# First queries in two loads by pairs of heads, the small term as a 33rd element, six idle products fewer

## The chip, the cores and the metric

The kernel runs on one core of a Trainium2 chip. A core has five engines that work side by side, each with a queue of its own: TensorE (PE in the profile; its weight loads are PEld), VectorE (DVE), ScalarE (ACT), GpSimd (POOL) and SyncE (SP), which here issues most of the transfers. Transfers run on 16 DMA engines. Data lie in SBUF, 128 partitions wide; products are written to PSUM, which has eight banks. The metric is the device time of one execution in microseconds (us), as the median of several runs.

## The reference

Inputs are q, k, v (8 batches, 8 heads, 576 positions, 64 wide), phi (the same, 32 wide) and the weights of a mixture of eight experts over rows of 512.

```
a    = exp(phi - max(phi));  a = a / (sum(a) + 1e-9)          # over the 32
k_m  = a^T k ;  v_m = a^T v                                    # 32 x 64 for each head
s    = q k_m^T / 8 ;  s = exp(s - max(s));  s = s / (sum(s) + 1e-9)   # over the 32
x    = s v_m                                                   # rows of all heads side by side: 4608 x 512
e    = argmax(x w_gate + bias[modality]) ;  g = softmax weight of e
out  = g * (relu(x w1[e]) w2[e])                               # 512 -> 1024 -> 512
```

So each batch first makes 32 "memory" keys and values for each head out of phi, k and v, then softens 576 queries against them, and the resulting rows pass an expert. The 1e-9 is what the text calls the small term.

## The kernel before, in words

**Tiling.** A batch has 8 heads; they are held as 2 groups (NG, on the two halves of the partitions) of 4 heads (HG, along the free dimension). The 576 positions of a head are 64 partitions times 9 columns (QC). The columns of a batch are worked on in two parts, RA = 4 columns and RB = 5 columns. The expert is guessed on the chip from the bias alone, so that its weights can be loaded early; where the guess proves wrong in the end, a slower path follows, which is not taken with these inputs. Products whose precision matters are made three times, from upper and lower halves of the operands (names ending in h and l).

**Order.** Each engine works strictly in the order in which the kernel wrote its instructions. That order is made by a small planner, `weave()`: a list of steps for attention and one for the experts, each step with its predecessors and with estimated times (`TAKES`). The steps of the first batch are laid down by `plan_first()` in a fixed sequence; a step of the kind "nothing" has no estimated time, and `nothing(n)` writes n products whose result nobody reads. Behind the start the planner mixes attention of the next batches into the products of the experts.

**The start.** Ahead of everything the kernel writes, in this order: the loads of phi (halves from SP and ACT), k, v and the first part of the first queries on SP's queue; on PE, `warm_small(BUSY[0])` (small products on a tile of zeros) and `warm(BUSY[1])` (large ones); and small fills on GpSimd. Then `plan_first()`:

- the maximum of phi (`heads_max`, L305), its transposition on PE (`mem_top`, `turn` at L147), the guess of the expert on VectorE (L211 to L217) and, from SP, the loads of w1, of w2, and of the rest of the first queries (`guess`, L218 to L238);
- `mem_exp` (L363 to L373): subtraction on VectorE and exponential on ScalarE, in three parts by columns;
- `spread_row` (L250), `mem_sums` (L384 to L387) on VectorE;
- `first_products(0)` (L428) on PE, the keys; `first_sums` (L439); `first_divide` (L448 to L465), which ends with the even halves on ScalarE;
- the transposition of the queries on VectorE, `q_turn` (L547), heads 0 and 1; `first_odd(0)` (L472), the keys; `q_turn`, heads 2 and 3; on PE `first_products(1)` (L428), the values;
- `first_keys` (two transpositions on PE, L147, and a copy on ScalarE, L526), `first_scores` (L574);
- `soften` for each of the two groups (L601 transposition out of PSUM, L605 maximum, L607 subtraction, L609 exponential) and `first_weights` (L642 sum, L643 small term, L644 reciprocal, L646 product, L650 transposition), then `first_split` (L656, L658);
- between them the value weights out of w1 (L740, L749, L754, L757, L762) and the first hidden tiles (`hidden`, L787, and `relu`, L800 and L804); after those the first outputs (L824), which need w2's halves (`first_w2`: L863 on ScalarE, L864 on GpSimd).

In VectorE's order the lines that matter are:

```
turns(0, 0, 9.5)                                   # q_turn, heads 0 and 1
add(("ko", 0), "ko0", [("kn", 0)], first_odd, 0)   # the keys
turns(0, 1, 11.0)                                  # q_turn, heads 2 and 3
```

The remaining columns of the first queries are turned later (L547 again, `turns(1, ...)`), ahead of the second `first_scores`.

Of the kernel before, what the change touches and what calls it, by code (L numbers as in the profile page):

```python
# [8 lines left out]
F32 = mybir.dt.float32  # L9
# [45 lines left out]
def attn_moe(ctx: ExitStack, tc: tile.TileContext, q, k, v, phi, mod_id, w_gate, mod_bias, w1, w2, out):  # L55
# [20 lines left out]
    HW = MAIN + 2 * QP  # L76
    SCALE = 1.0 / float(D) ** 0.5
    EPS = 1e-9
    BUSY = 92, 10

    FAR = float(1 << 20)

# [87 lines left out]
    def halves(src, b):  # L170
        return src[b].rearrange("(j g) (p c) d -> (g p) j (c d)", g=NG, c=QC)
# [7 lines left out]
    def load_queries(b, c0=0, n=QC):  # L179
        if b == 0:  # L180
            cols = slice(c0 * D, (c0 + n) * D)
            nc.sync.dma_start(q_sb[b % 2][:, :, cols], halves(q, b)[:, :, cols])
            return
        src = q[b].rearrange("(j g) (t x) (u d) -> g u j t x d", g=NG, t=BL, u=2)
        for g in range(NG):
            for u in range(2):
                p0 = QP * g + BL * u
                to = q_sb[b % 2][p0:p0 + BL].rearrange("t j (x d) -> t j x d", d=BL)
                for j in range(HG):
                    later.append((to[:, j], src[g, u, j]))  # L190
# [396 lines left out]
    def by_token(x, n, inner):  # L587
        return x[:, 0:2 * NG * n * inner].rearrange("p (g a c m) -> p g a c m", a=2, g=NG, c=n)

    def soften(b, part, step=None, groups=None):  # L590

        n = rows_of(part)
        if step in (None, 0) and groups in (None, 0):
            live["a", b, part] = by_token(wk.tile([P, 2 * NG * RB * M], F32, name="a", bufs=2), n, M)
            live["mx"] = by_token(wk.tile([P, 2 * NG * RB], F32, name="mx", bufs=2), n, 1)
        a, mx, sc = live["a", b, part], live["mx"], live["sc", b]
        for gs in groups_of(b, part) if groups is None else [slice(groups, groups + 1)]:
            x, m = (y[:, gs].rearrange("p g a c m -> p (g a c) m") for y in (a, mx))
            if step in (None, 0):
                for g in range(gs.start, gs.stop):  # L600
                    nc.vector.transpose(  # L601
                        a[:, g].rearrange("p a c m -> p a (c m)"), sc[g][:, :, RA * part * BL:(RA * part + n) * BL]
                    )
            if step in (None, 1):
                nc.vector.tensor_reduce(m[:, :, 0], x, axis=AX.X, op=ALU.max)  # L605
            if step in (None, 2):
                nc.vector.tensor_tensor(x, x, m.broadcast_to(list(x.shape)), op=ALU.subtract)  # L607
            if step in (None, 3):
                nc.scalar.activation(x, x, AF.Exp, scale=SCALE)  # L609
# [25 lines left out]
    def first_weights(g, step):  # L635
# [3 lines left out]
        n = 2 * RA  # L639
        if step == 0:  # L640
            sa, ra = (wk.tile([P, 2 * NG * RB], F32, name=y, bufs=2)[:, 0:n] for y in ("sa", "ra"))
            nc.vector.tensor_reduce(sa, x, axis=AX.X, op=ALU.add)  # L642
            nc.vector.tensor_scalar_add(sa, sa, EPS)  # L643
            nc.vector.reciprocal(ra, sa)  # L644
            ra = ra.rearrange("p (x o) -> p x o", o=1)
            nc.vector.tensor_tensor(x, x, ra.broadcast_to(list(x.shape)), op=ALU.mult)  # L646
            return
# [283 lines left out]
    def plan_first():  # L931
# [27 lines left out]
        add(("top", 0), "top0", [("max", 0)], mem_top, 0)  # L959
        add(("preferred",), "guess", [], preferred)  # L960
        add(("guess",), "guess", [], guess)
        nothing(1)
        add(("exp", 0), "first exp", [("top", 0)], mem_exp, 0)
        nothing(4)
        add(("known",), "nothing", [], spread_row)
        add(("sums", 0), "first sums", [("exp", 0)], mem_sums, 0)
        add(("k", 0), "k0", [("exp", 0)], first_products, 0, floor=9.0)
# [255 lines left out]
    with tc.manual_schedule():  # L1223
# [9 lines left out]
        load_queries(0, 0, RA)  # L1233
        warm_small(BUSY[0])
        warm(BUSY[1])
        nc.gpsimd.memset(ones_c, 1.0)
        ones_r = wk.tile([1, P], F32, name="ones_r")
        nc.gpsimd.memset(ones_r, 1.0)
# [133 lines left out]
```

## Time and profile before

| | |
|---|---|
| median of 3 runs | 391.02 us (390.63 to 391.76) |
| profiled execution | 391.15 us, span 389.0 us |
| PE busy | 376.1 us, 97% of the span |
| VectorE busy | 245.3 us, 63% |
| ScalarE busy | 140.5 us, 36% |
| GpSimd busy | 45.7 us, 12% |
| chain that ended last | PE 92%, DMA 3%, DVE 2% |
| mean granted clock of TensorE | 0.996 |

How to read the rows. A row of the timeline or of the chain starts with the start and the length in us, counted from the span's start, then engine, line of the kernel, operation, what it writes and reads, the shape and how often; in brackets the idle time of the engine ahead of it and what ended it. SPq and ACTq are the queues that issue transfers. A row of the transfers gives the size in KB and the us from issue to landing. A row of the windows gives the stretch, its length, for PE, PEld, DVE, ACT and POOL the busy us and the number of instructions, then PE's granted clock, the share of the DMA engines' time and GB/s. A row of waits gives who waited for whom, the us in total, how often and the longest. The time of an execution is longer than its span by what lies around it.

### The profile page before, as it was taken

How to read it: one execution, taken by the hardware profiler on the slowest of the kernel's cores; microseconds unless marked ns; L12 is line 12 of the kernel's file. 1: busy time of each engine (PE TensorE's matmuls, PEld its weight loads, DVE VectorE, ACT ScalarE, POOL GpSimd, SP SyncE). 2: the span in 40 equal slices, each digit the busy share in tenths (PEclk: the TensorE clock that was granted, in tenths of full speed). 3: DMA queues.
4: the chain of work that ended last, by engine and by line, in shares of the span. 5: the costliest groups of instructions: out<-in, count | busy, mean ns of one | idle time of the engine just before them, and what ended most of it. 6: DMA issues, size and time to landing. Idle time of an engine off the chain costs nothing.

```text
span 389.0 us, 9842 instructions
## 1 busy us (share of the span) xinstructions
PE 376.1 (97%) x3987; PEld 302.1 (78%) x3988; DVE 245.3 (63%) x613; ACT 140.5 (36%) x327; POOL 45.7 (12%) x112
## 2 busy tenths in 40 slices
PE   7899999999999999989999999999999999999992
PEld 3577876889679797877879877787968887798982
DVE  4788758867787397735686479654774635880400
ACT  2382423534335153423433334341543242441310
POOL 3247030040000300030000300021000030000000
PEclk9999999999999999999999999999999999999998
DMA  8998679978750588419611096816311010171111
GB/s 294 349 376 207 102 122 310 281 199 294 162 102 29 177 232 209 164 24 341 111 35 56 9 346 108 293 29 205 95 29 50 7 42 16 27 272 30 28 42 48
DMA packets 91451, 56.89 MB, mean 146 GB/s; under 512 B 69252, under 2 KB 74628, under 8 KB 91396
## 3 DMA queue, kind: packets, MB, share of 16 engines
q1 hardware_dynamic: 90976, 55.74, 51.0%
q8 instruction: 33, 0.54, 0.6%
q10 hardware_dynamic: 420, 0.43, 0.3%
q14 instruction: 22, 0.18, 0.1%
HBM read 37.28 MB, written 18.87 MB: 144 GB/s over the span
## 4 chain that ended last, share of the span: by engine, by line
PE 92%; DMA 3%; DVE 2%; issue 1%; ACT 0%; SPq 0%; ACTq 0%
PE pe L824 53%; PE pe L787 26%; PE pair L403 4%; PE pe L740 4%; DMA q_sb<-in_q_dram 3%; PE pair L556 2%; PE pair L687 1%; PE pair L574 1%; PE pair L147 1%; PE pair L536 0%; PE pair L411 0%; SPq L177 0%; DVE a L646 0%; DVE aT L650 0%; DVE mx L605 0%
## 5 line engine op out<-in xcount | busy, mean ns | idle before, releaser
L824 PE MATMUL pe<-w2h,hh 128*128 128x512 f32 x288 | 117.2, 407 | 0.0
L824 PE MATMUL pe<-w2h,hl 128*128 128x512 f32 x288 | 112.6, 391 | 0.0
L824 PE MATMUL pe<-w2l,hh 128*128 128x512 f32 x288 | 110.6, 392 | 0.0
L804 DVE SCALAR_TENSOR_TENSOR hl<-pe,hh 128x256 fp32r<-128x256 f32 (+2 forms) x158 | 57.5, 390 | 38.6 <-ACT hh L800 37.7
L824 PEld LDWEIGHTS pe<-w2h,hh 128*128 128x128 f32 x288 | 54.1, 188 | 23.8 <-issue 13.8
L800 ACT ACTIVATE hh<-pe 128x256 fp32r<-128x256 f32 (+2 forms) x158 | 53.2, 361 | 37.2 <-PE pe L787 36.5
L824 PEld LDWEIGHTS pe<-w2l,hh 128*128 128x128 f32 x288 | 54.0, 188 | 11.8
L824 PEld LDWEIGHTS pe<-w2h,hl 128*128 128x128 f32 x288 | 54.2, 188 | 9.4
L837 ACT ACTIVATE ob<-pe,gates 128x512 f32<-128x512 f32 x35 | 23.9, 687 | 76.4 <-PE pe L824 44.0
L787 PE MATMUL pe<-xbh,vwh 128*128 128x320 f32 x128 | 40.3, 315 | 0.0
L787 PE MATMUL pe<-xbh,vwl 128*128 128x320 f32 x128 | 39.6, 309 | 0.0
L787 PE MATMUL pe<-xbl,vwh 128*128 128x320 f32 x128 | 39.6, 309 | 0.0
L787 PE MATMUL pe<-xah,vwh 128*128 128x256 f32 x124 | 35.3, 287 | 0.9 <-ACT xah L656 0.9
L787 PE MATMUL pe<-xal,vwh 128*128 128x256 f32 x124 | 34.9, 283 | 0.0
L787 PE MATMUL pe<-xah,vwl 128*128 128x256 f32 x124 | 34.9, 283 | 0.0
L339 POOL COPY ts<-tm 32x4 f32<-32x4 f32 x24 | 4.8, 199 | 205.6 <-DVE tm L331 204.9
L787 PEld LDWEIGHTS pe<-xah,vwh 128*128 128x128 f32 x124 | 23.6, 192 | 3.2 <-ACT xah L656 2.0
L152 ACT CAST vwh<-pe 128x512 fp32r<-128x512 f32 x26 | 14.0, 590 | 32.1 <-PE pe L740 32.1
L787 PEld LDWEIGHTS pe<-xbh,vwh 128*128 128x128 f32 x128 | 24.0, 188 | 1.2 <-DVE hl L804 0.6
L787 PEld LDWEIGHTS pe<-xbl,vwh 128*128 128x128 f32 x128 | 24.1, 188 | 0.3
L787 PEld LDWEIGHTS pe<-xbh,vwl 128*128 128x128 f32 x128 | 24.0, 188 | 0.0
L787 PEld LDWEIGHTS pe<-xal,vwh 128*128 128x128 f32 x124 | 23.7, 192 | 0.2
(173 smaller groups left out, 440.6 us busy)
## 6 DMA issues: line engine op xcount, KB each, us to landing
kv_sb<-in_k_dram SPq DMA_DIRECT2D x8, 1152.0 KB, 6.9
kv_sb<-in_v_dram SPq DMA_DIRECT2D x8, 1152.0 KB, 9.2
out_dram<-ob SPq DMA_DIRECT2D x65, 128.0 KB, 2.6
q_sb<-in_q_dram SPq DMA_DIRECT2D x112, 72.0 KB, 3.1
ph<-in_phi_dram SPq DMA_DIRECT2D x7, 576.0 KB, 10.2
raw<-in_moe_w_dram SPq DMA_DIRECT2D x2, 1024.0 KB, 7.1
raw<-in_moe_w_dram SPq DMA_DIRECT2D x1, 1280.0 KB, 10.7
out_dram<-ob SPq DMA_DIRECT2D x3, 256.0 KB, 2.0
```

The costliest lines, as they stand in the source:

```text
L147: nc.tensor.transpose(dst, src, ident[:rows, :rows])
L152: nc.scalar.copy(h, src)
L339: nc.gpsimd.tensor_copy(ts_[BL * a:BL * (a + 1)], live["tm"][BL * o:BL * (o + 1)])
L403: nc.tensor.matmul(live["kvp"][M * j:M * (j + 1), g], lhsT=pe[half, j, c * M:(c + 1) * M], rhs=kv_sb[half, :, j, c * D:(c + 1) * D], start ...
L556: nc.tensor.matmul(sc[g][M * j:M * (j + 1), a, 0:QC * BL], lhsT=kvT[b][rows, 0, M * j:M * (j + 1)], rhs=qT[rows, j, a], start=True, stop=T ...
L574: nc.tensor.matmul(sc[g][M * j:M * (j + 1), a, c0 * BL:(c0 + n) * BL].rearrange("p (c t) -> p c t", t=BL), lhsT=kT0[p0:p0 + BL, u, M * j:M ...
L740: nc.tensor.matmul(pvs[g][M * j:M * (j + 1), :], lhsT=vT[b][rows, j, :], rhs=raw1[rows, j, cols], start=True, stop=not more, tile_position ...
L787: nc.tensor.matmul(ph[:, 0:n], lhsT=(vl if k == 2 else vh)[:, g, cols], rhs=xl if k == 1 else xh, start=(g == k == 0), stop=(g == NG - 1 a ...
L800: nc.scalar.activation(hs[0][:, f, h0:h0 + p1 - p0], live["ph", f][:, p0:p1], AF.Relu)
L804: nc.vector.scalar_tensor_tensor(hl, live["ph", f][:, p0:p1], 0.0, hh.bitcast(F32), op0=ALU.max, op1=ALU.subtract)
L824: nc.tensor.matmul(po, lhsT=tile_columns(hl if n == 1 else hh, f, t), rhs=(w2l if n == 2 else w2h)[:, f, :], start=(f == n == 0), stop=(f ...
L837: nc.scalar.activation(ob, po, AF.Copy, scale=gate_of(b, t))
```

## The change

Three things are changed in the start of the kernel; the order of all other instructions is left alone.

1. The first part of the first queries (4 columns of all heads) is loaded by two transfers in place of one: heads 0 and 1 of each group, then heads 2 and 3. The rest of these queries is loaded by one transfer as before.
2. The weights of the first part get a tile of their own, `a0`, 33 elements wide in place of 32. GpSimd fills the 33rd column with the small term at the start. The four steps of `soften` and the product and transposition of `first_weights` work on the first 32 columns; the sum runs over all 33, and the separate addition (L643) goes.
3. Six products of nothing go: one of the 92 small ones, one behind `preferred` and `guess`, four behind `mem_exp`, ahead of the keys.

```diff
-    BUSY = 92, 10
+    BUSY = 91, 10
...
         if b == 0:
             cols = slice(c0 * D, (c0 + n) * D)
-            nc.sync.dma_start(q_sb[b % 2][:, :, cols], halves(q, b)[:, :, cols])
+            for js in (slice(0, HG // 2), slice(HG // 2, HG)) if c0 == 0 else (slice(0, HG),):
+                nc.sync.dma_start(q_sb[b % 2][:, js, cols], halves(q, b)[:, js, cols])
             return
...
         if step in (None, 0) and groups in (None, 0):
-            live["a", b, part] = by_token(wk.tile([P, 2 * NG * RB * M], F32, name="a", bufs=2), n, M)
+            live["a", b, part] = live["a0"][:, :, :, :, 0:M] if b == part == 0 else by_token(
+                wk.tile([P, 2 * NG * RB * M], F32, name="a", bufs=2), n, M
+            )
...
                     nc.vector.transpose(
-                        a[:, g].rearrange("p a c m -> p a (c m)"), sc[g][:, :, RA * part * BL:(RA * part + n) * BL]
+                        a[:, g] if b == part == 0 else a[:, g].rearrange("p a c m -> p a (c m)"), sc[g][:, :, RA * part * BL:(RA * part + n) * BL]
                     )
...
             sa, ra = (wk.tile([P, 2 * NG * RB], F32, name=y, bufs=2)[:, 0:n] for y in ("sa", "ra"))
-            nc.vector.tensor_reduce(sa, x, axis=AX.X, op=ALU.add)
-            nc.vector.tensor_scalar_add(sa, sa, EPS)
+            whole = live["a0"][:, g].rearrange("p a c m -> p (a c) m")
+            nc.vector.tensor_reduce(sa, whole, axis=AX.X, op=ALU.add)
             nc.vector.reciprocal(ra, sa)
...
         add(("guess",), "guess", [], guess)
-        nothing(1)
         add(("exp", 0), "first exp", [("top", 0)], mem_exp, 0)
-        nothing(4)
         add(("known",), "nothing", [], spread_row)
...
         warm(BUSY[1])
+        live["a0"] = wk.tile([P, NG, 2, RA, M + 1], F32, name="a0")
+        nc.gpsimd.memset(live["a0"][:, :, :, :, M:M + 1], EPS)
         nc.gpsimd.memset(ones_c, 1.0)
```

## The prediction

> **What bounds the kernel now.** I read the page first, for its span, and then the waits of PE alone from 23.8 us to the end, to see whether anything behind the start can absorb or add time.
>
> ```profile
> span 389.0 us, 9842 instructions
> ```
>
> ```profile
> PE pair L411 <- issue: 1.3, 1, 1.3
> PE pe L787 <- ACT xah L656: 0.9, 1, 0.9
> ```
>
> In 365 us PE waits twice. One wait, at L787, is the end of the start: the last products of the first hidden tiles wait for the second group of first weights. The other (L411) is a pause of 1.3 us that no engine causes. All else is one unbroken row of products. So whatever reaches PE earlier at L787 arrives at the end in full, as long as no transfer that keeps its own time gets in between; a change ahead of L787 that isn't on the way to it is worth nothing.
>
> The way to L787 is read from the chain of waits in order of time (start, length, what):
>
> ```profile
> 2.29 11.05 DMA q_sb<-in_q_dram
> ...
> 14.77 0.44 PE pair L147 x2
> 15.24 0.38 ACT kT L526
> 15.66 1.05 PE pair L574 x54
> 16.74 0.46 DVE a L601
> ...
> 19.27 0.18 DVE sa L643
> 19.48 0.21 DVE ra L644
> ...
> 20.25 0.46 DVE aT L650
> ...
> 21.95 0.18 DVE sa L643
> 22.16 0.21 DVE ra L644
> ...
> 23.79 0.51 PE pe L787 x2
> ```
>
> It starts with the load of the first queries, landed at 2.29 + 11.05 = 13.34 us. Then come VectorE's transposition of the queries, the keys, the key transposition on PE (L147), its copy (L526), the scores (L574), and from 16.74 us VectorE without a pause worth naming. Both additions of the small term (L643) lie on this chain. Why the queries hold up the keys is in the timeline of that stretch:
>
> ```profile
> 11.38 0.29 DVE L387 TENSOR_TENSOR sums<-sums,t2top 128x128 f32<-128x128 f32 x1
> 11.73 0.29 PE L439 MATMUL pair<-ones_c,sums 64*64 64x1 f32 x8
> 11.88 2.20 PE L428 MATMUL pe<-kv_sb,exp 64*64 64x128 f32 x72
> ...
> 12.48 0.16 DVE L452 TENSOR_TENSOR recs<-rec,places 128x4 f32<-128x4 f32 x1
> 12.74 0.52 ACT L465 ACTIVATE even<-pair,recs 128x64 f32<-128x64 f32 x2 [2.46 <-DVE recs L452]
> 13.37 0.71 DVE L547 STREAM_TRANSPOSE q_sb<-q_sb 128x512 f32<-128x512 f32 x1 [0.72 <-DMA q_sb<-in_q_dram]
> ...
> 14.00 0.82 DVE L472 SCALAR_TENSOR_TENSOR keys<-pair,recs,even 128x64 f32<-128x64 f32 x4
> 14.73 0.70 DVE L547 STREAM_TRANSPOSE q_sb<-q_sb 128x512 f32<-128x512 f32 x1
> ```
>
> VectorE is free at 12.64 us, but next in its order is the transposition of heads 0 and 1, and that waits 0.72 us for the whole load of four heads. Behind it in the same queue stand the four key instructions, whose inputs (the even halves) are there at 13.26 us.
>
> **The split load.** The one transfer of 512 KB (128 partitions, 4 heads, 1 KB pieces) becomes two of 256 KB, in the same order on the same queue. What lies ahead of them stays as it is, and so does the total of bytes. The DMA engines are full in this stretch:
>
> ```profile
> 12.00:14.00 2.00, 2.00 (x75) 1.84 (x72) 1.12 (x4) 0.52 (x2) 0.00 (x0) 1.00 1.05 383
> ```
>
> At 383 GB/s (last column) half of the load, 0.262 MB, is 0.68 us. So heads 0 and 1 land at 12.66 us and heads 2 and 3 at 13.34 as before. The transposition then starts at 12.69 us (now, too, it starts 0.03 us behind the landing; VectorE is free at 12.64), against 13.37: **0.68 us** less. It hands over after 0.63 us (13.37 to 14.00), so the keys start at 13.32 us, just behind the even halves' 13.26; no more than 0.74 us could be had here. The second transposition comes at 14.05 us, 0.7 us behind its own landing. PE's key transposition moves from 14.77 to 14.09 us, where the value products, which end at 11.88 + 2.20 = 14.08 us, are just left behind: this is the next limit, and what is asked fits by 0.01 us. L526 and L574 follow at the same distance; L574 at 14.98 us finds the second half of the queries done at 14.05 + 0.70 = 14.75. The second issue stands on SP's queue right behind the first, where SP has nothing else to do until the choice of the expert (first issue after it at 9.31 us, below); it costs the path nothing there.
>
> [...]
>
> **The 33rd element.** The scores' first part gets a tile of its own, 33 wide, whose last column holds the small term; the sum then runs over 264 elements instead of 256 and L643 goes, once for each of the two groups. By the chain, L643 takes 19.27 to 19.48 and 21.95 to 22.16: 0.21 us each. Against it stands the longer sum:
>
> ```profile
> 18.83 0.41 DVE L642 TENSOR_REDUCE sa<-a 128x8 f32<-128x256 f32 x1
> ```
>
> Eight elements more are at most 8/256 of 0.41 us, 0.01 us. That leaves 0.20 us each, **0.40 us** together, both on the chain, the second because ScalarE and PE wait for it at L787. The transpositions, the maximum, the subtraction and the exponential now walk rows 33 apart. No row shows that step. The nearest are the two transpositions of the same size, one written as it comes (L601, 0.46 us) and one into a scattered order (L650, 0.46 us): no difference, so I take nothing. From the other side, if each of the seven VectorE passes of a group were 5% longer, the 0.40 us would shrink to about 0.1. The one new fill on GpSimd stands ahead of its other small fills, and the wait of GpSimd for the modality ids hides it; without that cover it would be one fill of 16 elements, which L643's 0.21 us bounds.
>
> **Six products of nothing fewer.** One of 92 small ones (0.01 us), one behind the transposition of the maxima, and four ahead of the keys' products. What bounds the path here is VectorE: the keys' sums end at 11.38 + 0.29 = 11.67 us and the sums' products (L439) start at 11.73. The keys' products stand in PE's order ahead of L439; if they begin earlier, PE waits for the same L387. Worth nothing, unless the array's clock suffers, which is a rival below.
>
> **What is late next.** Transfers keep their times while all else comes 1.08 us earlier. I compare each landing (issue plus time to landing) with its first user:
>
> ```profile
> 9.31 0.40 SPq L222 DMA_DIRECT2D raw<-in_moe_w_dram  x1
> ...
> 12.30 1.10 SPq L227 DMA_DIRECT2D raw<-in_moe_w_dram  x1
> ...
> 17.46 0.43 SPq L182 DMA_DIRECT2D q_sb<-in_q_dram  x1
> ```
>
> ```profile
> raw<-in_moe_w_dram SPq DMA_DIRECT2D x1, 1024.0 KB, 7.1
> ```
>
> ```profile
> raw<-in_moe_w_dram SPq DMA_DIRECT2D x1, 1280.0 KB, 10.7
> ```
>
> ```profile
> q_sb<-in_q_dram SPq DMA_DIRECT2D x1, 640.0 KB, 10.0
> ```
>
> ```profile
> 17.35 1.13 PE L740 MATMUL pair<-raw,kvT 64*32 64x512 f32 x16 [0.35 <-ACT kvT L531]
> 24.12 0.62 ACT L863 CAST w2h<-raw 128x512 fp32r<-128x512 f32 x1
> ...
> 27.80 0.84 DVE L547 STREAM_TRANSPOSE q_sb<-q_sb 128x640 f32<-128x640 f32 x1
> ...
> 28.86 0.82 DVE L547 STREAM_TRANSPOSE q_sb<-q_sb 128x640 f32<-128x640 f32 x1
> ...
> 30.59 1.18 PE L574 MATMUL pair<-q_sb,kT 32*32 32x160 f32 x64
> ```
>
> The first half of w1 lands at 16.4 us and is wanted at 17.35 - 0.68 = 16.67: in time by 0.2. The second half has no landing in the trace; w2's 1.31 MB behind it end at 23.0 us and take 3.4 us at 383 GB/s, so it is there at about 19.6 us, perhaps a few tenths late for its products (L740 again, further on). PE has 0.9 us to spare there, since it waits at L787 afterwards. w2 lands at 23.0 us and its first cast moves to 24.12 - 1.08 = 23.04: a tie. The rest of the first queries lands at 27.46 us, and VectorE would want it at 26.7. Here VectorE will **wait 0.75 us** at L547, with one lower half of the hidden tiles, the second transposition and a maximum of the next phi queued behind. The second transposition then ends at about 29.4 us (27.5 + 1.06 to its start + 0.82), and PE wants it for the scores at 30.59 - 1.08 = 29.5. So this wait is swallowed by a distance that shrinks from 0.9 us to 0.1; I charge 0.03 us and keep 0 to 0.3 for the range.
>
> **Sum.** 0.68 + 0.40 - 0.03 = 1.05 us. The profiled execution took 391.15 us (span 389.0 and 2.1 us around it) and would take 390.10; it lies 0.13 us above the median of the three runs, 391.02, so against that median the forecast is **389.97 us**.
>
> **Rivals.** First, *the halves don't part*: the transposition of heads 0 and 1 waits for both, or the first half's last engine lands late. [...] Against it: the rest of these queries shares the tile with them, lands at 27.46 us, and the transposition at 13.37 us doesn't wait for it. Only 0.40 us would be left: 390.6 us.
>
> Second, *the transfers take it back*: the landing at 27.46 us or w2's at 23.0 comes a few tenths later than now, or the wide rows cost their 5%. The distance left over is 0.1 us, so each further tenth goes straight into PE's scores. With 0.3 to 0.6 us lost it gives 390.3 to 390.6, say 390.4 us.
>
> Third, on the other side, *the clock of the array falls* in the pause that the missing products leave, and the products of keys and values run at half speed. The times of products of nothing and the busy time by window (PE first, clock the third column from the end):
>
> ```profile
> 3.12 3.62 PE L158 MATMUL pair<-busy 128*128 128x512 bf16 x8 [0.22 <-issue]
> ...
> 8.04 1.04 PE L158 MATMUL pair<-busy 128*128 128x512 bf16 x4
> ```
>
> ```profile
> 13.66:17.07 3.41, 2.17 (x83) 1.29 (x75) 2.60 (x9) 0.84 (x4) 0.19 (x2) 1.00 1.11 295
> 6.84:10.25 3.41, 2.99 (x40) 1.73 (x44) 2.70 (x9) 1.48 (x4) 0.69 (x7) 1.00 1.03 381
> ```
>
> Such a product starts every 0.43 us at first and every 0.22 us at 8 us, so the array was at half speed at first, whatever the clock column says of that time. Without the four (1.04 us) and the single one (about 0.25) the stretch from 6.84 to 10.25 us would have some 1.7 us of PE in place of 2.99, half, and a pause of about 1 us in one piece. For the rival: the row of 13.66 to 17.07 us, which stays fast, has more, 2.17 us, two thirds. Against it: that stretch, too, holds pauses of 0.7 and 0.45 us (14.08 to 14.77 and 15.21 to 15.66). If the clock fell, the keys' products, of the same number and form as the values', would take 4.4 instead of 2.20 us from about 9.4 (11.73 - 2.2) and end at 13.8; the values' products, at full speed again by then, would end at about 16.2 with L439 between, and the key transposition would start at 16.2 instead of 14.77. That is 1.4 us lost against 0.40 won: 391.02 + 1.0 = 392.0 us. It decides once the fall comes early enough to slow more than half of the keys' products, ahead of about 10.5 us.
>
> Fourth, *each transfer pays its own start in line*. The bound is the smallest transfer that the page lists alone:
>
> ```profile
> out_dram<-ob SPq DMA_DIRECT2D x65, 128.0 KB, 2.6
> ```
>
> Of its 2.6 us to landing, 0.131 MB at 383 GB/s are 0.34; if the other 2.3 us stood in line, the second half would land at 15.6 us, its transposition would end at 16.35, and the scores would start 0.7 us later than now: 391.02 + 0.7 - 0.40 = 391.3 us. Against it: the engines' share of 1.05 in the window above leaves no room for such gaps between the transfers that already stand in this queue. [...]
>
> **How the numbers follow.** The forecast gets 0.62, the halves that don't part 0.08, the transfers that take it back 0.16, the falling clock 0.09, the start in line 0.03, and 0.02 remain for a larger gain than I see. The forecast's own range is 389.5 to 390.3. The range reaches from there over the first two rivals, 389.4 to 391.0, and leaves the clock and the start in line out. A measurement of this kernel can tell about 0.3% from no change, 1.17 us: faster means below 389.85, slower above 392.19. The forecast lies only 0.12 us from that bound, so half of its 0.62 counts as faster: 0.31 + 0.02 = 0.33. Slower is 0.06 of the falling clock's 0.09, since it can hit a second stretch. The rest is no change, 0.61.
>
> **What would show it.** L547's first row would start near 12.69 us with a wait of less than 0.1, the keys at 13.32, L574 near 14.98. Each L644 (renumbered) would follow the sum directly, and L787's wait would end near 22.7. The load of the rest would show as a wait of about 0.75 us at L547 near 26.7, and PE would still have no other wait. The forecast is wrong if L787 moves by 1.1 us and the span doesn't, if the transposition still waits until 13.3, or if the products of the keys take longer than 2.2 us.

## The result, and the profile after

The changed kernel takes **389.34 us** (median of 5 runs, 388.08 to 389.78) against 391.02 us before: a ratio of 0.9946, 95% interval 0.9922 to 0.997. That is faster by 1.7 us where 1.05 were forecast, and below the range, which began at 389.4. Almost nothing of it came the way the prediction had it. In the rows below the lines are renumbered (L411 is L412, L428 is L429, L547 is L548, L642 is L646, L740 is L743, L787 is L790); the kernels of the experiments have numbers of their own, up to 10 apart.

The page of the changed kernel, and the waits of PE from 9 us on (who waited for whom, us in total, how often, longest):

```profile
span 387.9 us, 9830 instructions
...
PEclk9899999999999999999999999999999999999998
```

```profile
PE pair L429 <- ACT exp L374: 0.6, 1, 0.6
PE pair L575 <- ACT kT L527: 0.5, 1, 0.5
PE pair L743 <- ACT kvT L532: 0.4, 1, 0.4
```

The two waits that the prediction named are both gone: the 0.9 us at L787, and the pause of 1.3 us at L411, which no engine caused and which the prediction had held fixed. The second digit of the clock's row is an 8. The windows of that stretch (PE first, granted clock third from the end):

```profile
6.40:9.81 3.41, 1.83 (x26) 1.12 (x28) 2.70 (x10) 1.07 (x3) 0.98 (x8) 1.00 1.05 387
9.82:13.22 3.40, 3.40 (x79) 3.40 (x74) 1.68 (x5) 0.43 (x2) 0.00 (x0) 0.50 1.07 370
```

PE was busy for 1.83 of 3.41 us, and in the next 3.40 us its clock was half. The timeline of VectorE and PE in the start of the changed kernel:

```profile
9.31 3.69 PE L429 MATMUL pair<-kv_sb,exp 64*64 64x128 f32 x72 [0.62 <-ACT exp L374]
...
13.18 0.16 DVE L449 TENSOR_SCALAR den<-pair 128x2 f32<-128x2 f32 x1 [1.54 <-PE pair L440]
...
13.65 0.71 DVE L548 STREAM_TRANSPOSE q_sb<-q_sb 128x512 f32<-128x512 f32 x1
14.39 0.86 DVE L473 SCALAR_TENSOR_TENSOR keys<-pair,recs,even 128x64 f32<-128x64 f32 x4
...
17.77 1.09 PE L743 MATMUL pair<-raw,kvT 64*32 64x512 f32 x16 [0.35 <-ACT kvT L532]
...
19.26 0.42 DVE L646 TENSOR_REDUCE sa<-a 128x8 f32<-128x264 f32 x1
19.71 0.20 DVE L647 RECIPROCAL ra<-sa 128x8 f32<-128x8 f32 x1
...
22.46 0.50 PE L790 MATMUL pe<-xah,vwh 128*128 128x256 f32 x2
...
23.99 0.40 PE L790 MATMUL pe<-xah,vwh 128*128 128x256 f32 x2
```

The keys' products take 3.69 us in place of 2.20; VectorE waits 1.54 us for PE (L440), and the transposition of the first queries starts at 13.65 us, later than before (13.37), with no wait for a transfer. The row that stood at 23.79 us before, the first product on the second group of first weights, is at 23.99 us. So the start as a whole came out 0.2 us later, and the span is 1.1 us shorter all the same: the pause that is missing at 172 us took 1.34 us in the kernel before, whose timeline of PE reads there

```profile
172.34 0.28 PE L411 MATMUL pair<-ones_c,sums 64*32 64x1 f32 x15
173.96 0.16 PE L411 MATMUL pair<-ones_c,sums 64*32 64x1 f32 x1 [1.34 <-issue]
```

A further 0.3 us lies outside the span: the profiled executions took 391.15 us with a span of 389.0, and 389.74 us with 387.9.

The five runs don't agree as well as those of before. At mean granted clocks of 0.995 and 0.996 the shortest two have spans of 386.5 and 386.3 us; at 0.992 two have 387.9 and 388.0; the fifth, with 387.5 at 0.995, fits neither. Half a clock over 3.4 us takes 1.7 / 388 = 0.004 off the mean, so the lower mean fits executions in which the clock fell as in the profiled one; only the profiled ones show where it fell.

### The profile page after: what moved, and what is told of

Same layout as the page of the kernel before. It is cut to its first block, busy times and chain, and to the rows that moved or that the text cites. A ratio compares the mean times of both kernels' runs of the same rounds, so it can differ in the third digit from the quotient of the medians.

```text
span 387.9 us, 9830 instructions
## 1 busy us (share of the span) xinstructions
PE 377.1 (97%) x3982; PEld 303.0 (78%) x3982; DVE 245.2 (63%) x611; ACT 140.7 (36%) x327; POOL 45.7 (12%) x113
## 4 chain that ended last, share of the span: by engine, by line
PE 96%; DVE 1%; DMA 1%; ACT 0%; issue 0%; ACTq 0%
PE pe L827 53%; PE pe L790 26%; PE pe L743 4%; PE pair L404 4%; PE pair L557 2%; PE pair L690 1%; DMA ph<-in_phi_dram 1%; PE pair L429 1%; PE pair L147 1%; DVE top L306 1%; PE pair L575 1%; PE pe L429 1%; PE pair L743 1%; PE pair L537 0%; PE pair L790 0%; PE pair L412 0%
## 5 line engine op out<-in xcount | busy, mean ns | idle before, releaser
L827 PEld LDWEIGHTS pe<-w2h,hh 128*128 128x128 f32 x288 | 54.0, 188 | 22.7 <-issue 12.6
L790 PE MATMUL pe<-xbh,vwh 128*128 128x320 f32 x128 | 40.3, 315 | 0.0
L790 PE MATMUL pe<-xbh,vwl 128*128 128x320 f32 x128 | 39.5, 309 | 0.0
L790 PE MATMUL pe<-xbl,vwh 128*128 128x320 f32 x128 | 39.5, 309 | 0.0
L790 PE MATMUL pe<-xah,vwh 128*128 128x256 f32 x124 | 35.1, 286 | 0.0
L790 PE MATMUL pe<-xal,vwh 128*128 128x256 f32 x124 | 34.9, 283 | 0.0
L790 PE MATMUL pe<-xah,vwl 128*128 128x256 f32 x124 | 34.9, 283 | 0.0
L790 PEld LDWEIGHTS pe<-xah,vwh 128*128 128x128 f32 x124 | 23.6, 191 | 2.0 <-ACT vwl L760 0.8
L790 PEld LDWEIGHTS pe<-xbh,vwh 128*128 128x128 f32 x128 | 24.0, 188 | 1.3 <-DVE hl L807 0.6
L790 PEld LDWEIGHTS pe<-xbl,vwh 128*128 128x128 f32 x128 | 24.0, 188 | 0.3
L790 PEld LDWEIGHTS pe<-xbh,vwl 128*128 128x128 f32 x128 | 24.0, 188 | 0.0
L790 PEld LDWEIGHTS pe<-xal,vwh 128*128 128x128 f32 x124 | 23.7, 192 | 0.2
```

Of the source, the lines that this page charges most:

```text
L790: nc.tensor.matmul(ph[:, 0:n], lhsT=(vl if k == 2 else vh)[:, g, cols], rhs=xl if k == 1 else xh, start=(g == k == 0), stop=(g == NG - 1 a ...
L827: nc.tensor.matmul(po, lhsT=tile_columns(hl if n == 1 else hh, f, t), rhs=(w2l if n == 2 else w2h)[:, f, :], start=(f == n == 0), stop=(f ...
```

## The experiments

The theories, as they stood ahead of the runs. A: the load and the 33rd element are worth about what the forecast says, and the pause at L411 is PE's wait for the next piece of its instruction stream, so that it hangs on how many instructions stand ahead of it. B: the removed products were in the way. C: the transfers, by way of the split, did away with the pause. Each kernel was timed beside the kernel before.

### All products of nothing kept

The changed kernel with the load and the 33rd element only.

```diff
-    BUSY = 91, 10
+    BUSY = 92, 10
...
         add(("guess",), "guess", [], guess)
+        nothing(1)
         add(("exp", 0), "first exp", [("top", 0)], mem_exp, 0)
+        nothing(4)
```

> The split load and the 33rd element, with all products of nothing kept, so that PE has as many instructions as before. Theory A (the start gains 1.05 us by the load and the 33rd element; the rest of the gain is the pause of 1.34 us at the sums' products of the fifth batch, which hangs on where PE's instructions are cut into pieces of 16 KB for fetching): the start ends 1.05 us earlier (first product of the second group near 22.7 us), the pause at 172 us stays, 389.97 us, ratio 0.9973, no fall of the clock after 6.8 us. Theory B (the removed products themselves were in the way): about the same here, 390 us. Theory C (the further gain is the way fewer, later transfers fall, due to the split): the pause is gone and 388.6 us.

Measured: 389.86 us (389.23 to 392.6), ratio 0.996 (0.9941 to 0.998); profiled span 388.5, clock 0.996. Its timeline of VectorE and PE, and its waits of PE:

```profile
12.48 0.71 DVE L548 STREAM_TRANSPOSE q_sb<-q_sb 128x512 f32<-128x512 f32 x1
13.15 0.86 DVE L473 SCALAR_TENSOR_TENSOR keys<-pair,recs,even 128x64 f32<-128x64 f32 x4
...
16.54 1.09 PE L743 MATMUL pair<-raw,kvT 64*32 64x512 f32 x15 [0.35 <-ACT kvT L532]
18.51 0.59 PE L743 MATMUL pair<-raw,kvT 64*32 64x512 f32 x1 [0.88 <-issue]
...
21.71 0.50 PE L790 MATMUL pe<-xah,vwh 128*128 128x256 f32 x2
...
23.24 0.40 PE L790 MATMUL pe<-xah,vwh 128*128 128x256 f32 x2
```

```profile
PE pe L827 <- issue: 1.5, 1, 1.5
PE pair L743 <- issue: 0.9, 1, 0.9
```

Without the fall of the clock the load does what was forecast of it: the transposition starts 0.89 us sooner than the 13.37 of before, the keys 0.85. The pause at 172 us is there (1.5 us), which speaks for A and against C. But 0.81 us of head start at L743 (16.54 against 17.35) have become 0.55 us at the second group (23.24 against 23.79), because PE pauses for 0.88 us at 17.63 us, again for no engine. A had not seen that one coming. Its time of 389.97 us is nearly met, but not by the 1.05 us of the start that A names: 0.55 come from the start and 0.3 from outside the span, and the profiled execution took 390.36 us, 0.5 more than the median.

### The products alone

```diff
-    BUSY = 92, 10
+    BUSY = 91, 10
...
-        nothing(1)
...
-        nothing(4)
```

> Only the six products of nothing are taken out of the kernel before. Theory A: the pause of 1.34 us is gone; where the clock stays up 389.7 us; where it falls between 9.8 and 13.2 us the keys' products take 3.7 us, the key transposition waits for the values' products till 15.2 us in place of 14.77, and it takes 390.1 us. Theory B: 1.3 us gained, too, but with PE's pause at the fifth batch in place and the gain ahead of 24 us. Theory C: the pause stays, 391.0 to 391.5 us.

Measured: 389.98 us (389.71 to 391.59), ratio 0.9961 (0.9941 to 0.9981), profiled span 387.8. This kernel has neither the load nor the 33rd element, and its span is that of the changed kernel:

```profile
span 387.8 us, 9830 instructions
```

```profile
PE pe L740 <- issue: 0.2, 1, 0.2
```

Its page has the same 8 in the clock's row, and the wait of 0.2 us is the only pause without an engine behind 9 us. So taking out the six products, which the forecast put at nothing, both takes the pause away and brings the clock down.

### Twelve instructions fewer at the head

Six of the 92 tiny products (a product and its weight load each) are left away, all larger products of nothing kept: once in the kernel before, once in the kernel of the first experiment.

```diff
-    BUSY = 92, 10
+    BUSY = 86, 10
```

> The kernel before with six small products of nothing fewer at the very start (86 of 92), all large ones in place: PE has exactly as many instructions fewer as in the change, but nothing is missing ahead of the keys. Theory A (cut of the instruction stream): the pause at 172 us is gone, all else as before, 389.7 us, ratio 0.9966, clock up from 6.8 us. Theory B (the products themselves were in the way): 391.0 us, ratio 1.000, the pause in place. Theory C: the same 391.0 us.

> The split load and the 33rd element, the five large products of nothing kept, six small ones fewer at the very start. Theory A: start 1.05 us earlier, the pause at 172 us gone, the clock never falls: 388.6 us in every execution, ratio 0.994, better than the changed kernel's median of 389.34. Theory B: 390.0 us. Theory C: 388.6 us as well.

Measured: 390.96 us (ratio 0.9983, 0.997 to 0.9995) and 390.53 us (0.997, 0.9956 to 0.9983), clock up in both. The pause of 1.3 us at 172 us is gone in both, as A has it (0.2 us are left in the first, none in the second), though none of the larger products ahead of the keys was removed. But the time hardly moves, because two new pauses stand in the start: 1.0 us at L428 and 1.1 us at L740 in the first, 0.7 and 1.3 us in the second.

### The cut alone

Five of the tiny products fewer, and nothing else, in the kernel before.

```diff
-    BUSY = 92, 10
+    BUSY = 87, 10
```

> The kernel before with five of its 92 tiny products at the head fewer and nothing else: the instruction stream of TensorE is cut 10 instructions earlier, and its first wait lies at about its 195th instruction, still behind the end of the first piece at 192. Theory A (the pause at 172 us is the wait for a piece of the stream, and hangs on where the cut lies): it falls from 1.3 to 0.1 to 0.5 us, the start stays as in before (first product of the second group at 23.8 us), 389.9 to 390.3. Rival A' (the first wait so near to the cut brings the second piece late, as with six fewer): a pause of 0.7 to 1.0 us near 12.9 us, 390.5 to 391.0. Rival B (the pause has to do with what VectorE or a transfer does at 172 us): nothing changes, 391.0.

Measured: 391.1 us, ratio 0.999 (0.9979 to 1.0001). Rival A' holds, with 0.1 us more than it named: a pause of 0.77 us stands at 12.99 us, and the pause at 172 us has shrunk to 0.39 us. The first wait comes behind 193 instructions, not 195; the 192 of that expectation is its author's estimate, and the distances below put the end of the first piece at about 442 - 253 = 189. The stretches up to the pauses without an engine, for this kernel, for the kernel before, for the first experiment, and for the next one (from and to, length, then busy us and number of instructions, PE and its weight loads first):

```profile
0.00:12.99 12.99, 10.81 (x220) 6.18 (x222) 6.90 (x18) 3.30 (x7) 3.78 (x30) 1.00 0.88 315
0.00:19.51 19.51, 15.74 (x347) 8.72 (x348) 11.58 (x31) 5.80 (x15) 6.15 (x41) 1.00 0.94 322
0.00:174.74 174.74, 169.79 (x2117) 132.23 (x2119) 124.44 (x308) 68.37 (x156) 34.01 (x85) 1.00 0.72 201
```

```profile
0.00:172.62 172.62, 167.97 (x2117) 131.60 (x2119) 123.43 (x305) 67.78 (x154) 33.85 (x85) 1.00 0.73 203
```

```profile
0.00:17.63 17.63, 14.61 (x347) 8.54 (x349) 10.86 (x29) 4.98 (x13) 4.63 (x35) 1.00 0.94 317
0.00:172.09 172.09, 168.19 (x2118) 131.54 (x2119) 123.10 (x303) 67.79 (x154) 34.08 (x86) 1.00 0.73 204
```

```profile
0.00:18.74 18.74, 14.96 (x347) 9.79 (x349) 10.82 (x29) 4.95 (x13) 5.56 (x40) 0.91 0.94 321
0.00:172.73 172.73, 168.44 (x2118) 132.67 (x2119) 123.30 (x303) 67.91 (x154) 33.60 (x86) 0.99 0.73 203
```

Whatever was taken out or put in, and whenever it is, PE stops in these kernels behind one of the same numbers of instructions: 220 + 222 = 442, 695 or 696, and 4236 or 4237. The distances are 254 and 3541, which is 14 times 253. A pause of 0.4 us in the kernel with the load alone (below) stands behind 2468 instructions, about 7 times 253 ahead of 4237. The page of before says what comes in such portions:

```profile
PE 376.1 (97%) x3987; PEld 302.1 (78%) x3988; DVE 245.3 (63%) x613; ACT 140.5 (36%) x327; POOL 45.7 (12%) x112
...
q8 instruction: 33, 0.54, 0.6%
```

33 packets of 0.54 / 33 = 16.4 KB; over the 7975 instructions of PE and its weight loads 0.54 MB are 68 bytes each, some 240 to a packet. The records of this queue, set beside the moment at which PE goes on:

```
kernel                    packet starts   PE goes on   difference
before                       171.33         173.96        2.63
five tiny products fewer      11.20          13.76        2.56
five tiny products fewer      18.08          20.68        2.60
five tiny products fewer     172.52         175.13        2.61
```

In the other kernels of this study the difference is 2.3 to 2.6 us, in one case 3.0. So where PE paused for no engine, it went on 2.3 to 3.0 us after the transfer of a packet started. The reading of it is that PE's instructions had run out and the next piece wasn't there yet; the distances agree with the size (253 instructions against some 240 to a packet of 16.4 KB), and in the kernel before such a wait took 1.34 us.

### The changed kernel with the cut put back

Six tiny products more at the head of the changed kernel; nothing is put back ahead of the keys.

```diff
-    BUSY = 91, 10
+    BUSY = 97, 10
```

> The changed kernel with six more of the tiny products at its head (32 x 16, twelve instructions with their weight loads; they end ahead of TensorE's first wait, which is for VectorE and GpSimd): the cut of the instruction stream is again that of the kernel before, the work between the head and the keys that of the kernel after, the clock's fall included. Theory A (the 1.3 us gained came from the cut): the pause of 1.2 to 1.5 us at 172 us is back, and the time is 390.3 to 391.2, one microsecond or more above the changed kernel. Rival B (the products of nothing ahead of the keys were in the way): the time stays at 389.4, since none is put back there.

Measured: 390.72 us (389.65 to 392.09), ratio 0.9986 (0.997 to 1.0002); the changed kernel stood at 0.9944 to 0.9946 in its two comparisons. The waits of PE that no engine causes:

```profile
PE pe L827 <- issue: 1.3, 1, 1.3
...
PE pair L743 <- issue: 0.5, 1, 0.5
```

Six tiny products that stand ahead of a wait for other engines, and do no work, cost 1.3 us at 172 us. This settles it for A: the gain of the changed kernel was where the stream of instructions is cut, and B, for which nothing had changed here, falls.

### The changed kernel again, the load alone, the 33rd element alone

```diff
-            nc.sync.dma_start(q_sb[b % 2][:, :, cols], halves(q, b)[:, :, cols])
+            for js in (slice(0, HG // 2), slice(HG // 2, HG)) if c0 == 0 else (slice(0, HG),):
+                nc.sync.dma_start(q_sb[b % 2][:, js, cols], halves(q, b)[:, js, cols])
```

The second kernel is that of before with this edit only; the third has the tile `a0` of the change instead, with one load, and all products of nothing.

> The changed kernel once more, to be set beside the next three on one chip. Theory A (the products of nothing hold the clock: a window of 3.4 us that is 54% busy, as 6.40:9.81 was, ends in a half clock, and whether it falls depends on where the free-running windows lie): executions of two kinds, some at a mean granted clock of 0.991 to 0.993 with a span near 387.9 and some at 0.995 to 0.996 near 386.4; the time between 388.0 and 389.8. If the profiled one has the clock up, the first product of the second group starts at 22.7 to 22.9 us and not at 23.88. Rival B (the clock is a matter of the chip and not of the windows): all executions alike.

> The kernel before with the first queries loaded in two halves, all products of nothing kept and no 33rd element: the instruction stream of TensorE is cut as before. Theory A (0.68 us from the load, less what a starved TensorE takes near 17.6 us, and the pause at 172 us in place with 1.3 to 1.5 us): start of the first keys' product with the reciprocals about 0.7 us sooner than 13.37, L787's first wait ends 0.4 to 0.7 us sooner, 390.3 to 390.9. Rival: the 0.3 us that the changed kernels are shorter outside of the span come from the split load (time less span 1.83 here, 2.13 in the next kernel) or from the 33rd element (the other way round).

> The kernel before with the 33rd element alone: one load of the first queries, all products of nothing kept. Theory A (0.20 us a group fewer on VectorE, and nothing for the strided rows): the two groups' sums and the split of the second group 0.40 us sooner, 390.6 to 391.0, the pause at 172 us in place. Rival: strided rows cost VectorE something and the time stays at 391.4. Time less span as in the kernel above: 2.13 if the split load makes the 0.3 us outside of the span, 1.83 if the new tile does.

Measured: 389.44 us (387.92 to 389.77), ratio 0.9944 (0.9925 to 0.9964); 390.58 us, 0.9986 (0.9975 to 0.9996); 390.69 us, 0.9991 (0.9977 to 1.0005).

By the mean clock, two of the seven runs of the changed kernel held it (0.996 and 0.995; spans 386.1 and 386.4) and five didn't (0.991 to 0.993; 387.4 to 388.0), as A has it. With the first five runs that makes seven of 12 at 0.993 or lower; with only the six products removed it is six of eight, and in the kernel before 12 of the 84 runs that stood beside the experiments. So a low mean is common without the products and rare with them. The 23.88 us in that expectation should be the 23.99 of the row above.

In the load's kernel the timeline of PE, and in the element's kernel those of VectorE and PE:

```profile
18.68 0.59 PE L741 MATMUL pair<-raw,kvT 64*32 64x512 f32 x1 [1.03 <-issue]
...
23.42 0.44 PE L788 MATMUL pe<-xah,vwh 128*128 128x256 f32 x2
```

```profile
21.26 0.43 DVE L645 TENSOR_REDUCE sa<-a 128x8 f32<-128x264 f32 x1
21.72 0.20 DVE L646 RECIPROCAL ra<-sa 128x8 f32<-128x8 f32 x1
21.96 0.42 DVE L648 TENSOR_TENSOR a<-a,ra 128x256 f32<-128x256 f32 x1
...
23.35 0.51 PE L789 MATMUL pe<-xah,vwh 128*128 128x256 f32 x2
```

The load alone brings the second group 0.37 us forward (23.42 against 23.79), after a pause of 1.03 us; the 33rd element alone 0.44 us (the reciprocal at 21.72 against 22.16, the product at 23.35), of which 0.05 us were there ahead of the two sums. In the profiled execution what the load alone gains is lost again further on: at 92.1 us, behind 2468 instructions, PE pauses for 0.4 us that the profile of the kernel before doesn't have.

```profile
92.50 0.31 PE L788 MATMUL pe<-xbh,vwl 128*128 128x320 f32 x1 [0.40 <-issue]
```

The times of both kernels are as A has them, but a ratio of 0.9991 (0.9977 to 1.0005) doesn't tell the 33rd element from no change; its gain is read from the rows. The longer sum takes 0.42 and 0.43 us (0.41 before). Over rows 33 apart the first group's transposition takes 0.45 us, its maximum 0.42 and its subtraction 0.42, the same three times as in the kernel before: no cost of the stride shows. The two gains don't add up to the 0.55 us of the first experiment, because there PE itself had become the last to arrive.

The time outside the span is 2.12 us with the load alone and 1.79 with the 33rd element alone (medians of 12 runs each). So the 0.3 us go with the element, not with the load.

### The new tile, filled and not read

```diff
         warm(BUSY[1])
+        live["a0"] = wk.tile([P, NG, 2, RA, M + 1], F32, name="a0")
+        nc.gpsimd.memset(live["a0"][:, :, :, :, M:M + 1], EPS)
```

> The kernel before with the tile of 33 elements and GpSimd's filling of its last column alone: nothing reads it. The split load left the time outside of the span at 2.13 us, the 33rd element brought it to 1.79. Theory A (the tile and its filling do it): 1.79 here, and the time 0.3 below that of before, 390.7, with the same span. Rival (the two additions of EPS that VectorE no longer does): 2.13, and 391.0 as before.

Measured: 391.29 us, ratio 0.9999 (0.9987 to 1.001), 2.11 us outside the span. Neither the tile nor its filling makes the 0.3 us. By exclusion it is the two additions that VectorE no longer does, or the wider rows; no view of the profile shows what lies outside the span, and how either does it stays open.

### Holding the clock

The changed kernel with one product of nothing that is long and has few instructions, where TensorE waits for ScalarE anyway (0.62 us in the changed kernel); then the same with two tiny products fewer, so that the cut is exactly that of the changed kernel.

```diff
+    def long_nothing():
+        zeros = busy.bitcast(F32)
+        nc.tensor.matmul(
+            bank("pa"), lhsT=zeros[:, 0:P], rhs=zeros.rearrange("p (o c) -> p o c", o=1).broadcast_to([P, 2, 256]),
+            start=True, stop=True,
+        )
...
         add(("exp", 0), "first exp", [("top", 0)], mem_exp, 0)
+        add(("long",), "nothing", [], long_nothing)
```

```diff
-    BUSY = 91, 10
+    BUSY = 89, 10
```

> The changed kernel with one long product of nothing (128 x 512 in 32 bit, four instructions with its weight loads, some 0.86 us of TensorE by four times 0.21 us of the short ones) behind the exponents' spread, where TensorE waits for ScalarE anyway. Theory A (the clock falls for want of busy time in one window, and the stream of instructions is cut 8 instructions earlier than before rather than 12): the first window 79% busy, the clock never falls, the first keys' products take 2.20 us and not 3.69, first product of the second group near 22.8 us, no pause at 172 us; 388.0 to 388.4 in every execution. Rival B (products of nothing stand in the way of the keys): as slow as with all of them kept, 389.9. Rival C (four instructions are enough to move the cut back into a dense stretch): the pause of 1.3 us is back, 389.4 to 389.7.

> The kernel with the long product of nothing, and two of the tiny products at the head fewer, so that the instruction stream of TensorE is cut exactly as in the changed kernel (12 earlier than before, not 8). Theory A (what held the kernel with the long product at 388.83 is the pause of 0.45 us that its cut leaves at 172.8 us): no pause above 0.2 us behind 25 us, the clock up to the end, span 386.2 to 386.6, 388.0 to 388.4 and no second group of executions. Rival (the cut doesn't matter, the executions scatter by themselves): 388.8 as with the long product alone.

Measured: 388.83 us (388.43 to 390.25), ratio 0.9944 (0.9923 to 0.9965), with a pause of 0.45 us left at 172.8 us; then **388.23 us** (387.87 to 389.46), ratio 0.9922 (0.99 to 0.9943). By the mean clock the first kernel holds it in all six runs (0.995 to 0.997) but lies between A and C; a cut moved by 8 in place of 12 leaves a third of the pause. The second has the lowest median of the study, though its interval still touches those of the first and of the changed kernel; that its gain over the first is the 0.45 us is read from the traces. The page, windows, timeline of PE and waits of PE of the second:

```profile
span 386.6 us, 9829 instructions
```

```profile
5.74:9.15 3.41, 2.35 (x10) 0.69 (x8) 2.83 (x9) 0.46 (x1) 0.98 (x8) 1.00 1.04 392
9.16:12.56 3.40, 3.25 (x100) 2.95 (x104) 2.61 (x8) 1.05 (x4) 0.00 (x0) 1.00 1.07 372
```

```profile
16.77 1.09 PE L750 MATMUL pair<-raw,kvT 64*32 64x512 f32 x16 [0.36 <-ACT kvT L539]
...
18.89 1.08 PE L750 MATMUL pe<-raw,kvT 64*32 64x512 f32 x11 [0.22 <-issue]
...
23.11 0.40 PE L797 MATMUL pe<-xah,vwh 128*128 128x256 f32 x2
```

```profile
PE pair L582 <- ACT kT L534: 0.5, 1, 0.5
PE pair L750 <- ACT kvT L539: 0.4, 1, 0.4
PE pe L750 <- issue: 0.2, 1, 0.2
```

With 2.35 of 3.41 us busy the clock stays up, the second group starts at 23.11 us, 0.88 us ahead of the changed kernel (at 22.95 us in the first of the two), and no pause stands at 172 us. One of its six runs has a mean clock of 0.99 (389.46 us), which A had ruled out: with the product one of 12 runs has a low mean, without it seven of 12, so it makes the fall rarer and doesn't prevent it.

How far ScalarE's instructions lie from their times in the kernel before, at three moments of that kernel (us, negative is earlier), shows where each kernel gains:

```
kernel                                        26 us   140 us   260 us
load and 33rd element, products kept          -0.65    -0.54    -0.42
changed kernel                                +0.10    +0.18    -1.12
changed kernel with long product, same cut    -0.77    -0.81    -2.27
```

Between 140 and 260 us lies the pause at 172 us and nothing else that moves (the whole step is made between 168 and 182 us): -1.30 and -1.46 us where the cut is shifted by 12, +0.12 where it isn't.

## Why the prediction was wrong, point by point

**"A pause of 1.3 us that no engine causes", held fixed.** This is the step that failed. The page had the row (L411, released by "issue"), and the prediction took the pause for a constant and left it out of its sum. The change takes twelve instructions of PE away ahead of it; the pause was, by the counts, a wait for the next packet of 16.4 KB of the stream, and it went with the cut. Alone it is worth 1.34 us, more than the 1.1 by which the span fell.

**"Six products of nothing fewer ... worth nothing, unless the array's clock suffers."** Right in that no engine waited for them, wrong in the sum: their instructions moved the cut, and their work had held the clock. The chance of 0.09 for the falling clock was too low, with seven of 12 runs at the lower mean; the prediction had itself worked out 1.7 us of busy time for the window, and 1.83 were measured. The shape of the pauses was no comfort: the longest in that stretch was 0.62 us, and the clock fell all the same. Nor does the busy time of a window alone tell a fall from none. The clock's records put the windows 3.41 us apart; after the first of these two (the changed kernel with six tiny products more) it fell, after the second (the first experiment) it stayed up:

```profile
6.80:10.21 3.41, 2.10 (x43) 1.63 (x47) 2.80 (x9) 1.52 (x4) 0.63 (x6) 1.00 1.03 385
```

```profile
170.20:173.61 3.41, 1.90 (x153) 1.81 (x131) 1.29 (x4) 0.62 (x2) 1.07 (x3) 1.00 0.16 19
```

The window that kept the clock was the emptier one, and held a pause of 1.51 us. That the removed products bring the clock down is shown (a low mean in 13 of 20 runs of the changed kernel and of the products alone, in 12 of 84 of the kernel before); by what rule stays open.

**The price of that rival, 392.0 us.** Mechanism right, size wrong. The keys' products took 3.69 and not 4.4 us, since the clock fell only at 9.82 us, half a us into them (that makes 0.5 + 2 * 1.7 = 3.9; 0.2 us stay open; the prediction's start of 9.4 us should be 9.5, 11.73 - 2.2), and the start lost 0.88 us against the kernel with the long product, which held its clock (23.99 against 23.11), 0.20 against before. The rival put 1.0 us there. Half of the 2.7 us by which its time was missed is the pause at 172 us.

**The split load, 0.68 us.** Right where the clock holds. L547 was to start at 12.69, the keys at 13.32: measured 12.48 and 13.15 in the first experiment, 12.57 and 13.21 with the load alone. The halves part: each of them spans all the partitions, and with the load alone the first half's consumer started 0.80 us sooner (12.57 against 13.37). In the changed kernel itself the load was not what was waited for, because the keys' sums came at 13.18 us.

**The 33rd element, 0.40 us.** Right: 0.44 us at the second reciprocal, 0.39 without the 0.05 us that were there ahead of the sums, and no cost of the strided rows shows (0.45, 0.42 and 0.42 us for the first group's passes, as before). That it would also shorten the time outside the span by 0.3 us was not foreseen.

**"Whatever reaches PE earlier at L787 arrives at the end in full."** Behind L787 it held in the profile of the 33rd element alone, but not in that of the load alone, which lost its gain to the pause at 92.1 us. The step from VectorE to L787 failed: its wait was to end near 22.7 us, and the earliest start measured is 22.95 (the first kernel with the long product). PE's slack of 0.9 us ahead of L787 was spent on its way there. From L740's first product to L787's first it took 21.18 - 17.35 = 3.83 us before:

```profile
21.18 0.50 PE L787 MATMUL pe<-xah,vwh 128*128 128x256 f32 x2
```

It takes 21.71 - 16.54 = 5.17 us with load and element, 4.69 in the changed kernel. An earlier PE meets a piece of its stream that does not come earlier: its packet starts at 15.40 us before, at 16.00 in the first experiment and at 17.31 in the changed kernel. Of the 1.34 us more, 0.88 are the pause at 17.63 us, the rest lies in the products right behind it. Even the 33rd element alone meets it, at the same 695 instructions: the sixteenth product of its L742 starts 0.58 us behind the fifteenth (18.38 after 17.80), which the length of the products hides from the view of waits. So of the forecast's 1.05 us some 0.55 (first experiment) to 0.84 us (22.95 against 23.79) reach the second group.

**The wait of 0.75 us at L547 near 26.7.** It didn't come in the changed kernel, where the start was not earlier, and was 0.18 us in the kernel with the lowest median.

**Why 389.34, then.** Profiled against profiled: -1.34 us from the pause, +0.20 from the start with the clock down, -0.3 outside the span, together -1.44 against the 1.41 measured (391.15 to 389.74). The forecast's own two terms, 1.08 us, are hidden in the middle one. That the kernel came out faster, as forecast, is luck: nothing of these two terms reached the second group in it.

## What to carry to other kernels

A pause of PE that the profile puts down to "issue" need not be a constant; the one here took 1.34 us, 0.39 us with ten instructions fewer ahead of it, and 0.2 us or nothing with twelve fewer. So count the instructions ahead of such a pause, and if the pauses lie multiples of one number apart (about 253 here), expect an edit that adds or removes instructions ahead to move them, for better or worse: six tiny products put back cost 1.3 us here. Idle work ahead of a dense stretch may be what holds the clock; before it goes, sum PE's busy time over 3.4 us windows in every phase, as a warning and not as a rule: the four falls here came after windows with 1.83 to 2.10 us busy, and other windows with 1.90 to 2.17 us kept the clock. Where both matter, try few long instructions: here one long product, four instructions with its weight loads, held the mean clock in 11 of 12 runs and moved the cut by four.

## What the runs showed of the hardware that was not expected

- Where PE stops for no engine after the first 9 us, in all kernels profiled here, it is behind 442, 695 to 697, 2468 or 4236 to 4237 instructions, for 0.09 to 1.5 us, and it goes on 2.3 to 2.6 us (once 3.0) after a 16.4 KB packet of the instruction queue started. It stops at a given one of these places in some kernels and not in others.
- Dropping five or six tiny products at the head (10 or 12 instructions) brings two more such pauses into the start (0.77 and 1.17 us; 1.0 and 1.1 us), while two fewer than in the changed kernel do no such harm (with the long product, 0.22 us in all behind 9 us). In the first case PE's wait near 6.5 us comes behind 191 or 193 instructions, in all other kernels behind 197 or more, and the packet that PE needs behind 442 then starts at 11.20 to 11.29 us in place of 6.24 to 6.64. By the distance of 253, the piece before it ends at about 442 - 253 = 189, an estimate. What exactly triggers a packet stays open.
- The clock fell after windows that were 54, 54, 58 and 62% busy with no pause above 0.62 us, and stayed up after windows of 56% (with a pause of 1.51 us), 60, 61 and 64%. The windows lie at another phase in each execution (the first record of the full clock at 5.38 to 7.17 us), and the same kernel has the lower mean clock in some executions and not in others.
- The time outside the span is 2.1 to 2.15 us (medians) in every kernel with the additions of the small term on VectorE and 1.77 to 1.82 us in every kernel with the 33rd element.
